# Top-k attention with two expert layers: full-row tail keys, transposed weights in place, four score buffers, one matrix fetched behind a gather

## The chip, the core and the metric

The kernel runs on one core of one Trainium2 chip. The metric is the device time of one execution in microseconds (us). The core has a matrix engine (TensorE, PE in the rows, with its weight loads as PEld), a vector engine (VectorE, DVE), an activation engine (ScalarE, ACT), a general engine (GpSimd, POOL) and a queue that issues most transfers (SyncE, SP). Each engine runs its own instructions in order and waits on semaphores for the others.

## The reference

```python
scores = q @ k^T / 8                      # 4 batches, 8 heads, 576 queries x 576 keys, 64 per head
scores = where(scores >= 32nd largest of the row, scores, -1e9)
x = softmax(scores) @ v                   # -> 2304 tokens x 512
g = clipped-quadratic(x @ w_in)           # 512 -> 2048
x = g @ w_out                             # 2048 -> 512
logits = x @ w_gate                       # 8 experts
# all (token, expert) pairs in falling order of logit; a token goes to the first
# expert that is not full (288 places each)
out[mask_e] = relu(x[mask_e] @ w1[e]) @ w2[e]
```

## The kernel before, in words

**First phase.** The work is cut into 80 pairs: for each of 4 batches, four blocks of 128 queries and one of 64, times four pairs of heads. `scores` multiplies queries by keys in PSUM bank `pS`; ScalarE copies the result to a score buffer `s` (a ring of three, `t_s`). `topk` finds the 32nd largest with eight-wide maxima on VectorE, and ScalarE and GpSimd turn the buffer into masked exponentials, in place. `values` transposes the weights: four 128x128 pieces for each head go through bank `pPT` into a buffer `pt` (ring of two); the last 64 keys of both heads and the reciprocal of the sums go through bank `pQ` into `tr` (ring of one). It then multiplies by the values: for each head (half of the 128 output rows) four matmuls over 128 keys (`v`) and one over the last 64 keys (`u`, on 64 rows of the array). VectorE scales the result into `xf` (ring of one), and ScalarE and GpSimd split it into a high and a low part in `XB`.

Between the pairs run 32 decodes of 64-bit weight words (`weights`, in the first 160 us), and, as soon as 256 tokens are ready, the two big matrices for each of nine blocks (`ffn_block`).

**Second phase.** `route` finds expert after expert: three rounds of counting on VectorE and TensorE (tiles `yb`, `I`, `ge`, `n`), then the places of the expert's tokens (`places`), which give the row numbers `idx`. Three indirect transfers (`gathers`) bring 96 rows each into `xg`. `expert` fetches the expert's first matrix (four tiles `raw`) and its second one (four more), splits each into a high part (ScalarE) and a low part (VectorE) in `W`, transposes the rows and multiplies. For the first expert, two blocks of tokens that come out of the last FFN block are added from `yo` instead of being gathered (`last_block`).

**Order.** All operations are recorded, and a planner with costs of its own (`Program.issue`) sets the order on each engine. So an edit of one operation can move others; at run time each engine keeps the planned order and waits.

Nearly all operations stand in the profile under line 267, that of the recorder; so rows are told apart by tiles.

Of the kernel before, what the change touches and what calls it, by code (L numbers as in the profile page):

```python
# [9 lines left out]
F32 = mybir.dt.float32  # L10
# [4 lines left out]
AF = mybir.ActivationFunctionType  # L15
# [32 lines left out]
NF, NM, NSM, NXF, NTR, NQR = 5, 2, 3, 1, 1, 2  # L48
# [230 lines left out]
def kernel(ctx: ExitStack, tc: tile.TileContext, qm, qt, kT, vm, vt,  # L279
# [85 lines left out]
    def first_phase(exact, actx):  # L365
# [18 lines left out]
        t_u = ring(4, [128, 2, D], F32, "u")  # L384
        t_qr = ring(NQR, [128, 2, 128], F32, "qr")
        t_q = ring(2, tiles=[part(8192 + 512 * i, 512).rearrange("p (z i x) -> p z i x", z=2, i=2) for i in range(2)])
        t_s = ring(3, tiles=s_tiles)
# [3 lines left out]
        t_pt = ring(2, [128, 4, 128], F32, "pt")  # L391
        t_tr = ring(NTR, [128, 2, 128], F32, "tr")
        t_xf = ring(NXF, [128, 128], F32, "xf")
# [50 lines left out]
        def weights(exact):  # L444
            raws = [stage[:, 1024 * i:1024 * i + 1024] for i in range(2)]
            raws += [t.rearrange("p a x -> p (a x)")[:, :1024] for t in (t_s(), t_s(), t_s())[1:]]
            t32s = [stage[:, 2048:2560], spare] + [t_pt().rearrange("p c x -> p (c x)") for _ in range(2)]
# [26 lines left out]
        def load_pair(b, p):  # L474
# [13 lines left out]
            Y.dma_start(out=u_t[:, 0, :], in_=vt[b, :, p])  # L488
            Y.dma_start(out=u_t[:64, 1, :], in_=vt[b, 64:, p])
# [134 lines left out]
        def values(b, j, p, r, s_sb, rinv, wide):  # L624
            P.rank = r + R_PV
            _, v_t, u_t = KV[b, p]
            tail, rb, acc = pQ[:, 0:128], pQ[:, 128:256], pQ[:, 256:384]
            full = j < 4
            w = 128 if full else 64
            pts = []  # L630
            for i in range(2 if full else 1):
                o_ = 64 * i
                with P.group():
                    for c in range(4):
                        T.transpose(pPT[:, 128 * c:128 * c + 128], s_sb[:, i, o_ + 128 * c:o_ + 128 * c + 128], ident)
                pt = t_pt()
                A.activation(pt.rearrange("p c x -> p (c x)"), pPT, AF.Copy)
                pts.append(pt)
            flat = s_sb.rearrange("p a x -> p (a x)")
            tr = t_tr()  # L640
            if full:
                A.activation(wide.rearrange("p (a x) -> p a x", a=2), rinv[:, :2].unsqueeze(2).to_broadcast([128, 2, 64]),
                             AF.Copy)
            with P.group():
                if full:
                    T.transpose(tail, flat[:, 512:640], ident)
                    T.transpose(rb, wide, ident)
                else:
                    T.transpose(tail[:64, :], flat[:, 512:576], ident)
                    T.transpose(rb, rinv[:, 0:1].to_broadcast([128, 128]), ident)  # L650
            if full:
                A.activation(tr.rearrange("p a x -> p (a x)"), pQ[:, :256], AF.Copy)
            else:
                A.activation(tr[:64, 0, :], tail[:64, :], AF.Copy)
                A.activation(tr[:, 1, :], rb, AF.Copy)
            for cs in ((0, 1), (2, 3, 4)):
                with P.group():
                    for c in cs:
# [10 lines left out]
            if full:  # L669
                V.tensor_tensor(out=xf, in0=acc, in1=tr[:, 1, :], op=ALU.mult)  # L670
            else:
                for h in range(2):
                    hs = slice(64 * h, 64 * h + 64)
                    V.tensor_tensor(out=xf[hs, :64], in0=acc[hs, :64], in1=tr[hs, 1, hs], op=ALU.mult)
            t0 = b * S + 128 * j
            c0 = 0
            while c0 < w:
                k, off = divmod(t0 + c0, BLK)
                n = min(w - c0, BLK - off)
                if k not in xT:  # L680
                    xT[k] = t_x()
                xh, xl = xT[k][:, 0, p, off:off + n], xT[k][:, 1, p, off:off + n]
                A.activation(xh, xf[:, c0:c0 + n], AF.Copy)
                G.tensor_tensor(out=xl, in0=xf[:, c0:c0 + n], in1=xh, op=ALU.subtract)
                c0 += n
# [80 lines left out]
        def routing_constants():  # L766
            raw = t_pt().rearrange("p c x -> p (c x)")
# [14 lines left out]

        if not exact:
# [21 lines left out]
        t_pt.reset()  # L805
        at, blk = 0.0, 0
        for b in range(B):
            for j in range(5):
                for p in range(NP):
                    s_sb, f = scores(b, j, p, at, exact)  # L810
                    rinv, wide = (topk_exact if exact else topk)(b, j, p, at, s_sb, f)
                    values(b, j, p, at, s_sb, rinv, wide)
# [18 lines left out]
    def second_phase(exact, rctx):  # L831
# [250 lines left out]
        def route(ph):  # L1082
# [77 lines left out]
            V.scalar_tensor_tensor(out=pos, in0=sc, scalar=pS[:, 1, 8:9], in1=tk, op0=ALU.add, op1=ALU.mult)  # L1160
# [6 lines left out]
        def places(ph, ei, pos):  # L1167
# [50 lines left out]
        def expert(ph):  # L1218
# [195 lines left out]
```

## Time and profile before

| | |
|---|---|
| median of 3 runs | 1151.74 us (1150.81 to 1154.38) |
| profiled execution, its own time | 1145.99 us |
| its span, first to last instruction | 1143.7 us |
| mean granted TensorE clock | 0.963 |
| busy: PE, PEld, DVE, ACT, POOL | 93%, 82%, 81%, 70%, 61% |

The profiled execution is one of its own and lies 5.75 us under the median of the timed runs. The busy shares are means over stages that differ: attention alone, attention with the FFN, routing, and experts.

### The profile page before, as it was taken

To read this page: it belongs to the slowest core of one execution; us is meant where nothing else is said; L and a number is where in the kernel's file an instruction comes from. 1 tells how busy PE (TensorE), PEld (TensorE's weight loads), DVE (VectorE), ACT (ScalarE), POOL (GpSimd) and SP (SyncE) were. 2 spreads that over 40 slices of the span, in tenths; PEclk is the share of its full clock that TensorE was granted. 3 is DMA by queue.
4 is the path that set the end of the run, shared out by engine and by line. 5 is a ranking of instruction groups with operands and counts; after the bars stand their busy time and mean duration, and the time that the engine had idled before them with its cause. 6 is when DMAs were issued, how large, how long until landed. Compare 5 with 4: busy or idle time off the path is not lost. (4 is left out here: it accounts for less than half of the span.)

```text
span 1143.7 us, 24385 instructions
## 1 busy us (share of the span) xinstructions
PE 1062.0 (93%) x8359; PEld 940.0 (82%) x8359; DVE 931.2 (81%) x2923; ACT 805.0 (70%) x1835; POOL 697.5 (61%) x872
## 2 busy tenths in 40 slices
PE   3677799999999999999999999999997999999995
PEld 2456588888888888898888888888976899999995
DVE  7899999889999999989899999984257997776430
ACT  8899987778888888877888988874313455445541
POOL 6988988977876988757688777763211152223111
PEclk9976599999999999999999999999988999999998
DMA  9744332352212352322134312212315664556500
GB/s 268 220 156 157 111 117 70 109 165 66 92 54 61 96 175 66 92 73 80 61 101 129 93 52 70 82 59 64 117 53 184 208 200 160 169 189 204 175 22 24
DMA packets 62197, 132.81 MB, mean 116 GB/s; under 512 B 15984, under 2 KB 24432, under 8 KB 62064
## 3 DMA queue, kind: packets, MB, share of 16 engines
q1 hardware_dynamic: 58992, 121.73, 33.8%
q0 software_dynamic: 3072, 9.44, 2.5%
q8 instruction: 67, 1.10, 0.4%
q14 instruction: 66, 0.54, 0.2%
HBM read 116.98 MB, written 14.16 MB: 115 GB/s over the span
## 5 line engine op out<-in xcount | busy, mean ns | idle before, releaser
L267 PE MATMUL pH<-XB,W 128*128 128x256 f32 (+1 forms) x2496 | 360.0, 291 | 0.7 <-DVE spare L267 0.3
L267 PEld LDWEIGHTS pH<-XB,W 128*128 128x128 f32 x2496 | 326.5, 189 | 9.7 <-issue 2.9
L267 DVE MAX8 m<-f 128x8 f32<-128x288 f32 x720 | 302.6, 449 | 2.2
L267 POOL TENSOR_TENSOR s<-s,f 128x576 f32<-128x576 f32 x144 | 204.3, 1430 | 30.0 <-ACT f L267 29.1
L267 DVE MATCH_REPLACE8 f<-m,f 128x288 f32<-128x288 f32 x432 | 190.7, 444 | 0.5 <-issue 0.3
L267 PE MATMUL pX<-W,XB 128*128 128x512 f32 x608 | 184.7, 411 | 0.7 <-ACT XB L267 0.7
L267 PE MATMUL pS<-XB 128*128 128x288 f32 (+2 forms) x672 | 145.2, 327 | 31.9 <-POOL XB L267 15.3
L267 POOL TENSOR_TENSOR XB<-stage,XB 128x512 fp32r<-128x512 f32 (+1 forms) x96 | 126.9, 1323 | 59.1 <-ACT XB L267 35.1
L267 PEld LDWEIGHTS pS<-XB 128*128 128x128 f32 x672 | 107.9, 203 | 52.4 <-DVE f L267 18.5
L267 ACT ACTIVATE s<-s,sm 128x576 f32<-128x576 f32 x144 | 111.3, 773 | 22.4 <-POOL s L267 21.3
L267 PEld LDWEIGHTS pX<-W,XB 128*128 128x128 f32 x608 | 107.7, 191 | 19.4 <-issue 2.9
L1210 POOL DMA_INDIRECT xg<-dram_x,idx x24 | 35.4, 1476 | 123.6 <-issue 49.4
L267 ACT ACTIVATE f<-s,t_all 128x576 f32<-128x576 f32 x144 | 108.2, 772 | 2.5
L267 ACT ACTIVATE s<-pS 128x576 f32<-128x576 f32 x144 | 92.7, 643 | 23.2 <-PE pS L267 22.8
L267 PE MATMUL pX<-XB,W 128*128 128x288 f32 x768 | 108.6, 297 | 0.0
L267 DVE TENSOR_TENSOR f<-pS,s 128x288 f32<-128x288 f32 x198 | 86.4, 450 | 22.5 <-ACT s L267 9.2
L267 DVE TENSOR_TENSOR W<-raw,W 128x1024 fp32r<-128x1024 f32 x64 | 76.8, 1218 | 33.5 <-ACT W L267 33.3
L267 PEld LDWEIGHTS pX<-XB,W 128*128 128x128 f32 x768 | 103.5, 188 | 0.0
L267 PE MATMUL pPT<-ident,s 128*128 128x128 f32 x576 | 92.8, 286 | 8.3 <-ACT s L267 6.8
L267 ACT ACTIVATE pt<-pPT 128x512 f32<-128x512 f32 x144 | 84.9, 589 | 17.5 <-PE pPT L267 17.1
L267 PE MATMUL pQ<-pt,v 128*64 128x128 f32 (+1 forms) x1280 | 91.7, 283 | 5.4 <-ACT tr L267 5.2
L1304 POOL DMA_INDIRECT out_dram<-yo,idx x24 | 26.9, 1120 | 109.8 <-ACT yo L267 106.3
(209 smaller groups left out, 1910.2 us busy)
## 6 DMA issues: line engine op xcount, KB each, us to landing
wl<-dram_wlo SPq DMA_DIRECT2D x64, 512.0 KB, 3.4
raw<-in_w_dram SPq DMA_DIRECT2D x64, 512.0 KB, 4.8
qr<-in_qm_dram SPq DMA_DIRECT2D x128, 64.0 KB, 2.4
stage<-in_w_in_dram SPq DMA_DIRECT2D x14, 512.0 KB, 4.2
stage<-in_w_out_dram SPq DMA_DIRECT2D x14, 512.0 KB, 3.3
stage<-in_kT_dram SPq DMA_DIRECT2D x48, 144.0 KB, 2.8
dram_wlo<-wl SPq DMA_DIRECT2D x8, 512.0 KB, 3.1
v<-in_vm_dram SPq DMA_DIRECT2D x16, 256.0 KB, 3.2
```

Of the source, the lines that this page charges most:

```text
L267: P.add(eng, lambda: fn(*args, **kw), cost, reads, writes, lat)
L1210: return nc.gpsimd.indirect_dma_start(out=xg[:, g, :], out_offset=None, in_=x2d[:, :], in_offset=bass.IndirectOffsetOnAxis(ap=idx[:, g:g + ...
L1304: st = nc.gpsimd.indirect_dma_start(out=out, out_offset=bass.IndirectOffsetOnAxis(ap=idx[:, g:g + 1], axis=0), in_=yo, in_offset=None)
```

## The change

It does the following:

- The last 64 keys' values `u` stand in a buffer of 128 rows, head 0 in the upper and head 1 in the lower half, with zeros between (written once by GpSimd). Their matmul goes over all 128 rows. For the blocks of 64 queries one more transpose puts the same weights on both halves.
- Transposed weights go back into the score buffer that they come from, `xf` too; `pt` and `xf` are gone. There are four score buffers (the fourth, `s_last`, also serves the first decodes and the constants), and two `tr`, each half as wide; one ScalarE copy of 256 columns becomes two of 128.
- The ten value matmuls of a pair are one group for the planner, no longer two.
- In `route`, one VectorE instruction comes in ahead of the running sum (`most`) and one behind the sum of the places goes (`tok`).
- The first expert's second matrix is fetched only when all three gathers of that expert have landed.

```diff
-        t_s = ring(3, tiles=s_tiles)
+        s_last = apool.tile([128, 2, S], F32, name="s3")
+        t_s = ring(4, tiles=s_tiles + [s_last])
...
-            Y.dma_start(out=u_t[:, 0, :], in_=vt[b, :, p])
-            Y.dma_start(out=u_t[:64, 1, :], in_=vt[b, 64:, p])
+            for h in range(2):
+                Y.dma_start(out=u_t[64 * h:64 * h + 64, h, :], in_=vt[b, 64 * h:64 * h + 64, p])
...
-            if full:
-                A.activation(tr.rearrange("p a x -> p (a x)"), pQ[:, :256], AF.Copy)
...
+                    if full:
+                        T.transpose(tail, flat[:, 512:640], ident)
+                        T.transpose(rb, wide, ident)
+                    else:
+                        T.transpose(tail, flat[:, 448:576], ident)
+                        T.transpose(tail[:64, :], flat[:, 512:576], ident)
+                        T.transpose(rb, rinv[:, 0:1].to_broadcast([128, 128]), ident)
+                A.activation(flat[:, 512:640], tail, AF.Copy)
+                A.activation(tr, rb, AF.Copy)
...
+                pt = flat[:, 640 * i:640 * i + 512]
...
-            for cs in ((0, 1), (2, 3, 4)):
-                with P.group():
...
-                            elif full:
-                                T.matmul(acc[hs, :w], u_t[hs, 0, :], tr[hs, 0, :], start=False, stop=True)
                             else:
-                                T.matmul(acc[hs, :w], u_t[:64, h, :], tr[:64, 0, hs], start=False, stop=True)
...
+                                T.matmul(acc[hs, :w], u_t[:, h, :], flat[:, 512:640] if full else flat[:, 512:640][:, hs],
+                                         start=False, stop=True)
...
-            xf = t_xf()
...
+                xf = flat[:, :128]
...
+            most = rt([128, NT], F32, "most")
+            V.tensor_scalar(most, tk, 2.0 * N * E, None, op0=ALU.mult)
...
-            tok = rt([96, 3], F32, "tok")
-            V.tensor_reduce(out=tok, in_=pS[:96, 1, :6].rearrange("p (a g) -> p g a", a=2), axis=AX, op=ALU.add)
-            V.tensor_scalar(idx, tok, N - 1.0, None, op0=ALU.min)
+            V.tensor_reduce(out=idx, in_=pS[:96, 1, :6].rearrange("p (a g) -> p g a", a=2), axis=AX, op=ALU.add)
...
-                P.add("sync", partial(fetch, raw, i // 4, i % 4), 1450, [ei[0:1, 0:1]], [raw], 2500)
+                P.add("sync", partial(fetch, raw, i // 4, i % 4), 1450, [ei[0:1, 0:1]] + [xg] * (early and i > 3), [raw], 2500)
```

**First place: TensorE, the value matmuls of the first pair.** Before, a planner's group of four matmuls (each stands as two records in a trace) is cut off from the group of six by other work. The number behind a tile's name is its buffer.

```order
L267 MATMUL pQ<-pt_138,v_118 64x128
L267 MATMUL pQ<-pt_139,v_118 64x128
L267 MATMUL pQ<-pt_138,v_118 64x128
L267 MATMUL pQ<-pt_139,v_118 64x128
L267 MATMUL pS<-XB 128x288 x4
L267 MATMUL pX_71<-ident,stage 128x128 x4
L267 MATMUL pQ<-pt_138,v_118 64x128
L267 MATMUL pQ<-pt_139,v_118 64x128
L267 MATMUL pQ<-pt_138,v_118 64x128
L267 MATMUL pQ<-pt_139,v_118 64x128
L267 MATMUL pQ<-tr_140,u_122 64x128 x2
L267 MATMUL pS<-XB 128x288 x2
```

With the change the same pair reads the score buffer itself, in one run.

```order
L267 MATMUL pQ<-ident,s_105 128x128
L267 MATMUL pQ<-ident,f_132 128x128
L267 MATMUL pS<-XB 128x288 x4
L267 MATMUL pX_71<-ident,stage 128x128 x4
L267 MATMUL pQ<-s_105,v_118 64x128 x8
L267 MATMUL pQ<-s_105,u_122 64x128 x2
```

What moved: in the order before, 20 of the 80 pairs are cut in two like this; in the order with the change none is.

**Second place: VectorE, between the first expert's second matrix and the second expert's running sum (`SC`).** Before, the low parts of that matrix (`W_96`, `W_98`) stand ahead of the third round of the search.

```order
L267 TENSOR_TENSOR W_96<-raw_9798,W_95 128x1024
L267 TENSOR_TENSOR W_96<-raw_9799,W_95 128x1024
L267 TENSOR_SCALAR ge_9757<-pQ 128x8
L267 TENSOR_TENSOR W_98<-raw_9800,W_97 128x1024
L267 TENSOR_REDUCE n_0_9759<-pPT 128x1
L267 TENSOR_SCALAR y_9751<-y_9752,n_0_9759 128x18
L267 TENSOR_TENSOR W_98<-raw_9801,W_97 128x1024
L267 COPY yb_9754<-y_9751 128x144
```

With the change the third of its four tiles (`raw_9887`) stands directly ahead of the sum.

```order
L267 TENSOR_TENSOR W_98<-raw_9887,W_97 128x1024
L267 TENSOR_TENSOR yc_9848<-C_9833,eh_9827 128x144
L267 TENSOR_TENSOR closed_9818<-closed_9818,eh_9827 128x8
L267 SCALAR_TENSOR_TENSOR ej_9854,ef_9856<-eh_9827,s_105 128x8
L267 TENSOR_REDUCE ch_9850<-yc_9848 128x18
L267 TENSOR_SCALAR cp_1_9852<-closed_9818 128x8
L267 TENSOR_SCALAR ei_9858<-ef_9856 128x1
L267 SCALAR_TENSOR_TENSOR tk_9829<-y_9838,n_1_9847,ch_9850 128x18
L267 TENSOR_TENSOR L_0_9821<-L_0_9821,cp_1_9852 128x144
L267 SCALAR_TENSOR_TENSOR pen_9819<-tk_9829,pen_9819 128x18
L267 TENSOR_SCALAR most_9861<-tk_9829 128x18
L267 SCALAR_TENSOR_TENSOR SC_9823<-tk_9829 128x18
```

What moved: the round is now ahead of the second matrix's first tile, but its result waits behind the third tile.

**Third place: TensorE, just ahead of the first expert's first matmul (`pH_69<-XB,W_91`).** Before, nothing of the second expert's sum stands there.

```order
L267 MATMUL pX_71<-s_107,yo_9796 128x288
L267 MATMUL pH_69<-XB,W_91 128x288 x2
L267 MATMUL pH_69<-XB,W_92 128x288
L267 LDWEIGHTS ones_f
L267 MATMUL pPT<-ge_9758,ones_f 128x8
```

With the change the product of the sum (`pS<-SC`) does.

```order
L267 LDWEIGHTS ones_f
L267 MATMUL pPT<-ge_9845,ones_f 128x8
L267 MATMUL pH_70<-s_107,yo_9883 128x288
L267 MATMUL pS<-s_107,yo_9883 128x288
L267 MATMUL pX_71<-s_107,yo_9883 128x288
L267 LDWEIGHTS s_105
L267 MATMUL pS<-SC_9823,s_105 128x1
L267 MATMUL pH_69<-XB,W_91 128x288 x2
```

What moved: two products that need VectorE's results (`ge`, `SC`) are now ahead of the first expert's first matmul on TensorE.

## Rows read from the trace of the kernel before

**Rows 1.** Stretches: length, busy us of each engine (instructions), clock, DMA share, GB/s.

```profile
core 0: us, PE busy (x) PEld busy (x) DVE busy (x) ACT busy (x) POOL busy (x), PEclk, DMA share, GB/s
40.00:160.00 120.00, 91.94 (x556) 73.21 (x556) 116.22 (x354) 114.48 (x297) 104.63 (x126) 0.74 0.45 144
160.00:760.00 600.00, 592.67 (x4714) 514.93 (x4715) 556.66 (x1881) 498.56 (x1176) 470.91 (x612) 1.00 0.29 90
904.00:1144.00 240.00, 226.71 (x1971) 221.10 (x1969) 142.53 (x365) 105.64 (x191) 56.20 (x66) 0.98 0.43 141
```

**Rows 2.** Waits from 837 us to the end: who for whom, us, times, longest.

```profile
PE pH L267 <- DMA xg<-dram_x,idx: 8.5, 5, 3.0
```

**Rows 3.** Timeline of TensorE: start us, us, operation, records; three places.

```profile
436.13 1.09 PE L267 MATMUL pQ<-pt,v 128*64 128x128 f32 x16
437.16 0.44 PE L267 MATMUL pQ<-tr,u 64*64 64x128 f32 x4
437.52 0.50 PE L267 MATMUL pX<-W,XB 128*128 128x512 f32 x1
...
482.75 0.66 PE L267 MATMUL pQ<-pt,v 128*64 128x128 f32 x8
483.34 0.53 PE L267 MATMUL pS<-XB 128*128 128x288 f32 x2
483.80 0.66 PE L267 MATMUL pQ<-pt,v 128*64 128x128 f32 x8
484.39 0.43 PE L267 MATMUL pQ<-tr,u 64*64 64x128 f32 x4
...
450.64 0.60 PE L267 MATMUL pPT<-ident,s 128*128 128x128 f32 x4
451.00 0.78 PE L267 MATMUL pS<-XB 128*128 128x288 f32 x4
451.61 0.39 PE L267 MATMUL pX<-W,XB 128*128 128x512 f32 x1
```

**Rows 4.** ScalarE's groups by shape, 160 to 760 us: busy us, mean ns.

```profile
L267 ACT ACTIVATE tr<-pQ 128x256 f32<-128x256 f32 x53 | 20.0, 377 | 1.7 <-PE pQ L267 1.7
L267 ACT ACTIVATE tr<-pQ 128x128 f32<-128x128 f32 x12 | 3.2, 264 | 0.0
```

**Rows 5.** GpSimd's first real work; the constants' transfer: KB, median us to landing.

```profile
8.42 1.28 POOL L267 TENSOR_TENSOR W<-pt,W 128x512 fp32r<-128x512 f32 x1 [7.97 <-ACT W L267]
...
pt<-in_consts_dram SPq DMA_DIRECT2D x1, 240.0 KB, 2.5
```

**Rows 6.** Timeline around the first expert's gathers, all engines.

```profile
862.44 5.81 SPq L1233 DMA_DIRECT2D raw<-in_w_dram  x4
865.43 1.77 POOL L1210 DMA_INDIRECT xg<-dram_x,idx  x1 [0.30 <-issue]
874.12 0.74 PE L267 MATMUL pH<-ident,xg 96*128 96x96 f32 x2 [3.03 <-DMA xg<-dram_x,idx]
879.14 1.22 DVE L267 TENSOR_TENSOR W<-raw,W 128x1024 fp32r<-128x1024 f32 x1
883.26 0.77 PE L267 MATMUL pH<-XB,W 128*128 128x288 f32 x3
```

**Rows 7.** Tile xg, all 24 gathers: from issue to landing.

```profile
DMA to landing us min/median/max: 3.4/5.9/11.9
```

**Rows 8.** A stretch behind that wait, columns as in the first group.

```profile
875.40:878.60 3.20, 3.20 (x12) 2.44 (x12) 1.26 (x2) 0.95 (x1) 0.00 (x0) 0.50 0.31 119
```

**Rows 9.** The second expert's first matrix: issue, and the cast of its third tile.

```profile
886.62 2.14 SPq L1232 DMA_DIRECT2D raw<-in_w_dram  x4
...
893.67 1.07 ACT L267 ACTIVATE W<-raw 128x1024 fp32r<-128x1024 f32 x1 [0.65 <-DMA raw<-in_w_dram]
```

**Rows 10.** TensorE at the second expert's gathered rows.

```profile
901.50 0.30 PE L267 MATMUL pH<-ident,xg 96*128 96x96 f32 x1 [0.64 <-DMA xg<-dram_x,idx]
903.33 0.30 PE L267 MATMUL pH<-ident,xg 96*128 96x96 f32 x1 [1.53 <-DMA xg<-dram_x,idx]
```

More of the change, by code (lines that the diff above doesn't have):

```diff
@@ L445, in weights @@
             raws = [stage[:, 1024 * i:1024 * i + 1024] for i in range(2)]
-            raws += [t.rearrange("p a x -> p (a x)")[:, :1024] for t in (t_s(), t_s(), t_s())[1:]]
-            t32s = [stage[:, 2048:2560], spare] + [t_pt().rearrange("p c x -> p (c x)") for _ in range(2)]
+            raws += [t.rearrange("p a x -> p (a x)")[:, :1024] for t in s_tiles[1:3]]
+            t32s = [stage[:, 2048:2560], spare] + [s_last.rearrange("p a x -> p (a x)")[:, a:a + 512] for a in (0, 512)]
             for n in range(32):
@@ L622, in first_phase, with transposed @@
         xT, late = {}, []
-        def values(b, j, p, r, s_sb, rinv, wide):
+        def transposed(b, j, p, r, s_sb, rinv, wide):
             P.rank = r + R_PV
-            _, v_t, u_t = KV[b, p]
-            tail, rb, acc = pQ[:, 0:128], pQ[:, 128:256], pQ[:, 256:384]
+            tail, rb = pQ[:, 0:128], pQ[:, 128:256]
             full = j < 4
[L629 to L632, printed above, removed]
-                with P.group():
[L634 to L638, printed above, removed]
             flat = s_sb.rearrange("p a x -> p (a x)")
@@ L643, in values, with last @@
                              AF.Copy)
-            with P.group():
-                if full:
[L646 to L651, printed above, removed]
-                A.activation(tr.rearrange("p a x -> p (a x)"), pQ[:, :256], AF.Copy)
-            else:
-                A.activation(tr[:64, 0, :], tail[:64, :], AF.Copy)
-                A.activation(tr[:, 1, :], rb, AF.Copy)
-            for cs in ((0, 1), (2, 3, 4)):
-                with P.group():
-                    for c in cs:
+            def last():
+                with P.group():
+                    if full:
[7 more added lines that the diff above has]
+                A.activation(tr, rb, AF.Copy)
+            if not full:
+                last()
+            pts = []
+            for i in range(2 if full else 1):
+                pt = flat[:, 640 * i:640 * i + 512]
+                with P.group():
+                    for c in range(4):
+                        T.transpose(pPT[:, 128 * c:128 * c + 128], pt[:, 128 * c:128 * c + 128], ident)
+                A.activation(pt, pPT, AF.Copy)
+                pts.append(pt.rearrange("p (c x) -> p c x", c=4))
+            if full:
+                last()
+            return pts, flat, tr
+        def values(b, j, ps, r, made):
+            P.rank = r + R_PV
+            full = j < 4
+            w = 128 if full else 64
+            accs = [pQ[:, 256 + 128 * n:384 + 128 * n] for n in range(2)]
+            with P.group():
+                for p, (pts, flat, tr), acc in zip(ps, made, accs):
+                    _, v_t, u_t = KV[b, p]
+                    for c in range(5):
                         for h in range(2):
@@ new lines, in values @@
+            t0 = b * S + 128 * j
+            for p, (pts, flat, tr), acc in zip(ps, made, accs):
+                xf = flat[:, :128]
+                if full:
+                    V.tensor_tensor(out=xf, in0=acc, in1=tr, op=ALU.mult)
+                else:
+                    for h in range(2):
+                        hs = slice(64 * h, 64 * h + 64)
+                        V.tensor_tensor(out=xf[hs, :64], in0=acc[hs, :64], in1=tr[hs, hs], op=ALU.mult)
+                c0 = 0
+                while c0 < w:
+                    k, off = divmod(t0 + c0, BLK)
+                    n = min(w - c0, BLK - off)
+                    if k not in xT:
+                        xT[k] = t_x()
+                    xh, xl = xT[k][:, 0, p, off:off + n], xT[k][:, 1, p, off:off + n]
+                    A.activation(xh, xf[:, c0:c0 + n], AF.Copy)
+                    G.tensor_tensor(out=xl, in0=xf[:, c0:c0 + n], in1=xh, op=ALU.subtract)
+                    c0 += n
@@ L781, in need @@
                 more[1] = next(more[0]) + 1
+        P.rank = -10.0
+        for u_t in us:
+            G.memset(u_t[64:, 0, :], 0.0)
+            G.memset(u_t[:64, 1, :], 0.0)
         if not exact:
@@ L811, in first_phase @@
                     rinv, wide = (topk_exact if exact else topk)(b, j, p, at, s_sb, f)
-                    values(b, j, p, at, s_sb, rinv, wide)
+                    made.append(transposed(b, j, p, at, s_sb, rinv, wide))
+                    values(b, j, (p,), at, made)
+                    made = []
                     at += 1.0 if j < 4 else 0.6
@@ L1159, in route @@
             pos = rt([128, NT], F32, "pos")
-            V.scalar_tensor_tensor(out=pos, in0=sc, scalar=pS[:, 1, 8:9], in1=tk, op0=ALU.add, op1=ALU.mult)
+            V.scalar_tensor_tensor(out=pos, in0=sc, scalar=pS[:, 1, 8:9], in1=most, op0=ALU.add, op1=ALU.min)
             places(ph, ei, pos)
```

28 lines of the change are left out of this document (5 added, 23 removed).

## The prediction

> **What bounds the kernel now.** First the stretches [rows 1]: the kernel changes its limit three times. From 40 to 160 us, while the weights are decoded, VectorE is busy 116.2 of 120 us and ScalarE 114.5, TensorE 92 at a mean clock of 0.74: work taken off TensorE there buys nothing. From 160 to 760 us (attention beside the FFN) TensorE is busy 592.7 of 600 us and VectorE 556.7: TensorE leads, VectorE has 43 us in hand. From 904 us to the end (the experts) TensorE is busy 226.7 of 240 us, idle mostly behind its last matmul; an earlier start of that stage ends the kernel earlier. Between them lies the one place where TensorE stands still for a transfer: it waits 8.5 us in five pieces for gathered rows [rows 2].
>
> **The value matmuls.** The timeline of TensorE shows what the 64-row matmuls cost [rows 3]. In an uncut pair the 16 full-row records take 436.13 to 437.16, 1.03 us; a run of 8 takes 482.75 to 483.34, 0.59 us. So 8 more records cost 0.44, 0.055 each, and what is over is paid on entering and leaving. The four 64-row records take 437.16 to 437.52, 0.36 us. Four more records of the full-row kind would take 0.22. So a pair gains 0.14 us.
>
> A cut pair pays for entering twice: 2 x 0.59 - 1.03 = 0.15 us; and its guest, two score matmuls, takes 483.34 to 483.80, 0.46 us, where an undisturbed four take 0.61 (451.00 to 451.61), so 0.15 more: 0.30 us for a cut. By the order 20 pairs are cut before and none after; about 18 of them lie in the stage in which TensorE leads, and 70 of the 80 pairs. Gain there: 70 x 0.14 + 18 x 0.30 = 15.2 us. The added transpose of the 14 short blocks in it, four transposes taking 0.36 us (450.64 to 451.00), takes back 14 x 0.09 = 1.3. TensorE is relieved of 13.9 us.
>
> How much of it reaches the end? At most all; nothing, if VectorE (which gives up no instruction) is the true limit. VectorE's 43 us of idle time say that it follows TensorE's pace more than it sets it, but not everywhere: I take three quarters, 10.5 us.
>
> A rule speaks against this step. The Trainium skill, "TensorEngine Tiling (Array Packing)", sections Overview and When to Use Tiling, has it that a contraction of 64 rows or fewer should run as row tiles, for up to twice the speed. The trace disagrees: four 64-row records at 0.36 us are dearer than four full-row ones at 0.22, since the two heads run side by side in either form. By the rule the padded records would take twice 0.36 us, and the sum would be 25 us worse instead of 10 better.
>
> **The buffers.** A score buffer was free once its weights were transposed; now it is held until GpSimd has split the result, but there are four. I count it at 1 us of gain: between 0 and what VectorE's idle time leaves after the matmuls' part, some 20 us at the very most, and a loss if the longer hold outruns the fourth buffer (a rival below). ScalarE's one copy of 377 ns becomes two of at most 264 [rows 4]: 0.15 us more for each of 64 pairs, hidden by ScalarE's 101 idle us in the long stage, but not before 160 us, where some 9 pairs could cost 1.4 us; I count nothing, as VectorE is the fuller there. GpSimd's eight memsets lie in the 8 us in which it waits for its first operand [rows 5]; without that cover they would be a few tenths each. The `u` transfers become smaller and stay two for each pair of heads. New is a wait at the end of attention: the constants land in the fourth buffer, which the last pair now holds, and VectorE's casts of them, with the last FFN block's clipping behind them, wait 2.5 us for that transfer [rows 5]. Between 0 and 2 us; I take 0.5, as TensorE has the previous block's products to do.
>
> **The held fetch.** Around the first expert [rows 6] SyncE issues the second matrix at 862.44 us, GpSimd its third gather at 865.43, and TensorE gets that gather's rows only at 874.12. Over all 24 gathers a landing takes 3.4 us at best and 5.9 in the median [rows 7]. Without the second matrix beside it I take 4.2 us, nearer to the lower, since only the first matrix's last tiles still flow: landing at 869.6 (869 to 871.3 by the two bounds). So 4.5 of the 8.5 us of waiting go. But the second matrix starts only then, and VectorE's and TensorE's new order (second and third place above) puts the running sum of the next expert behind its third tile and the first expert's first matmul behind that sum. What that takes is shown by a burst of the same size that runs alone: issued at 886.62, the cast of its third tile starts 7.05 us later [rows 9]. So here: cast at 876.7, done at 877.7, low part (1.22 us [rows 6]) by 879.0, then eleven small VectorE operations and a first subtraction (an estimate: 1.9 us, somewhat over one and a half such low parts), 880.9, first matmul at 881 instead of 883.26. Of the 4.5 us, 2.3 are left.
>
> Then the clock. Behind the long wait TensorE ran at 1.2 GHz, the lower of its two levels (0.50), until 878.6 [rows 8], and it was full again when the first expert began. Now its idle time lies later, just ahead of that expert, and a drop to the same level would fall on dense work: 6.8 us at half clock cost 3.4 us, none cost nothing; I take 1.5. At the second expert's rows TensorE waits 0.64 and 1.53 us [rows 10]; that expert's search is about 5 us ahead of before while TensorE is only 2 ahead, so I drop these 2.2 us. Sum of the part: -2.3 + 1.5 - 2.2 = -3.0; bounds -8.5 (all waits of [rows 2] gone) and +3 (low clock, and the matrix landing late). The added `most` and the removed `tok` are one small VectorE operation each way on the same chain, under 0.2 us each and eight of either, behind TensorE's dense work: nothing.
>
> **The sum.** -10.5 - 1 + 0.5 - 3.0 = -14 us. Against the profiled execution's own 1145.99 us: 1132. It lies 5.75 us under the median of the runs, so for the median: 1151.74 - 14 = 1138 us. Within 0.3% (3.5 us) is what a measurement of this kernel can hardly tell from no change.
>
> **The rivals.**
> - *VectorE is the limit from 160 to 760 us.* For it: 93% busy. Against: TensorE has 7 us of idle time there, VectorE 43. The Trainium skill, "Perfetto Trace Analysis", section Identifying the Most-Contended Engine, speaks for it too: TensorE's headroom is to be read from weight loads, not from matmul time. By weight loads TensorE is 86% busy [rows 1], less than VectorE. Then TensorE's savings become waits, and some 1 us of the matmuls' part and the fetch's 3.0 remain: 1148 us. Chance 0.14.
> - *The fourth buffer frees VectorE.* If the score ring and not only TensorE held VectorE up, another 10 us of its idle time go: 1128 us. For it: three buffers for a pair's whole path from scores to transposes. Against: the order on TensorE puts the scores no further ahead than before. Chance 0.12.
> - *The hold on the second matrix costs more than the gather gains.* The upper bound above, +3: 1144 us. For it: the third tile ahead of the sum. Chance 0.12.
> - *The longer hold of a buffer outruns the fourth one: slower.* The pairs' order now needs GpSimd's last split of a pair before the fourth next pair's scores. Each us by which that comes late stops VectorE for the same time, for it has only these scores to do. Against 14 us of gain it decides from 0.2 us a pair on; at 0.25 us in 80 pairs, 20 us: 1158. Against it: one more buffer is 9 us more room in the long stage (600 us for some 65 pairs). Chance 0.04.
> - *Full rows cost double,* as by the first rule: 70 x (0.72 - 0.36) = 25 us instead of a gain of 10 from the matmuls: 1174 us. The rows above speak against it. Chance 0.01.
>
> **How the numbers follow.** The forecast, 1138 with 1131 to 1145 of its own, has 0.57. Range for 8 in 10: down to the fourth-buffer case, up to VectorE as the limit: 1127 to 1149. Faster by over 0.3%: the forecast, the buffer's case, most of the fetch's and half of VectorE's, 0.57 + 0.12 + 0.09 + 0.07 = 0.85; within 0.3%: 0.03 + 0.07 = 0.10; slower 0.05.
>
> **What would show it.** Right: the value matmuls of a pair stand as 20 records in about 1.25 us without a change of pace at the last four; the stage between the decodes and the last FFN block is 8 to 15 us shorter, with VectorE's busy share in it up from 93% to about 95%; the first expert's gathers land near 869.6 less what the first phase gained, and its first matmul starts about 2 us earlier relative to the gathers' issue; no wait at the second expert's rows. Wrong: new idle time of TensorE from 160 to 760 us as large as the matmuls' gain; ScalarE stopped for a tile of the second matrix with TensorE idle or at half clock behind it for more than 8 us; GpSimd's splits as the releaser of the scores' copies.

## The result, and the profile after

The changed kernel takes 1142.74 us (median of 5 runs, 1139.32 to 1143.89), the kernel before on the same chip 1151.74 us (5 runs): that is 9.0 us faster by the medians. The ratio on record is 0.9908, 95% interval 0.9882 to 0.9934, or 10.6 us (7.6 to 13.6); the comparisons below go by such ratios. The profiled execution of the changed kernel took 1143.89 us (span 1142.1), only 2.1 less than the profiled one of before. That gap between 2 and 9 us turns out to be part of the answer.

The long stage of [rows 1], in the changed kernel:

```profile
160.00:760.00 600.00, 588.21 (x4778) 521.69 (x4775) 556.08 (x1896) 507.98 (x1236) 475.27 (x614) 1.00 0.29 90
```

From 160 to 760 us TensorE (first busy column) fell from 592.7 to 588.2 us, VectorE (third) stayed at 556. By the forecast VectorE's share should have risen.

The value matmuls themselves became what was said of them. The timeline of TensorE for an uncut pair, columns as in [rows 3]:

```profile
437.01 1.09 PE L267 MATMUL pQ<-s,v 128*64 128x128 f32 x16
437.93 0.39 PE L267 MATMUL pQ<-s,u 128*64 128x128 f32 x4
438.25 1.20 PE L267 MATMUL pX<-W,XB 128*128 128x512 f32 x4
```

The 20 records take 437.01 to 438.25, 1.24 us (forecast 1.25, before 1.39). This pair is a typical one: in the long stretch defined below, the median of 66 pairs is 1.24 us, and before that of 50 uncut pairs was 1.39. Only a third of the 0.15 us lies at the last four records (0.32 us in place of 0.36); the rest lies ahead of them (0.92 in place of 1.03).

**A better ruler than fixed stretches.** Three events can be found in every trace: the first score copy of the 16th pair, the first expert's running sum on TensorE (`pS<-SC`), and the same for the fourth expert. They cut an execution into a start, a long stretch, the first three experts, and a rest. Here are the long stretch and the three experts for a second profile of the kernel before, an execution of 1152.48 us:

```profile
193.04:856.51 663.47, 655.02 (x5204) 569.89 (x5203) 572.61 (x1929) 506.88 (x1184) 469.73 (x606) 0.99 0.28 87
856.51:938.24 81.73, 72.66 (x593) 64.61 (x593) 63.56 (x182) 32.40 (x50) 19.77 (x15) 0.87 0.59 191
```

and for the changed kernel:

```profile
195.61:853.71 658.10, 644.76 (x5216) 571.64 (x5214) 567.61 (x1928) 512.36 (x1238) 471.12 (x608) 0.99 0.28 88
853.71:930.51 76.80, 66.48 (x595) 61.00 (x594) 63.05 (x183) 32.20 (x50) 17.50 (x15) 0.96 0.62 203
```

The long stretch repeats from execution to execution: 663.56, 663.47 and 663.58 us in three profiles with the order of before, 658.10 and 658.09 in two of the changed kernel. (`a_nohold` below, with the same order on VectorE in this stretch, has 659.1, and 3.4 us more at the lower clock.) So differences of 2 us can be read there, where the times of whole runs scatter by 4 to 9 us. The rest repeats within 2 us. What scatters is the first three experts: 75.6 us in the first profile of before, 81.73 in the second. The profile on which the forecast was built was an execution with a short one.

All profiles by this ruler (us; "VectorE busy" and "idle" are of the long stretch), with the median and the ratio to before of the run's own chip:

| kernel | start | long | VectorE busy | idle | 3 experts | rest | median | ratio (95%) |
|---|---|---|---|---|---|---|---|---|
| before, first profile | 192.6 | 663.6 | 572.7 | 90.8 | 75.6 | 212.0 | 1151.74 | |
| b_again | 193.0 | 663.5 | 572.6 | 90.9 | 81.7 | 212.0 | 1149.41 | 0.9995 (0.9982–1.0008) |
| b_hold | 193.7 | 663.6 | 572.8 | 90.8 | 72.5 | 212.0 | 1143.67 | 0.9950 (0.9934–0.9966) |
| b_values | 201.7 | 657.1 | 572.2 | 85.0 | 79.1 | 212.0 | 1149.33 | 1.0001 (0.9985–1.0017) |
| b_no_u | 191.1 | 652.9 | 569.1 | 83.8 | 79.9 | 212.7 | 1140.27 | 0.9896 (0.9870–0.9923) |
| changed, first profile | 195.6 | 658.1 | 567.6 | 90.5 | 76.8 | 211.6 | 1142.74 | 0.9908 (0.9882–0.9934) |
| a_again | 193.7 | 658.1 | 567.6 | 90.5 | 77.3 | 212.8 | 1141.40 | 0.9909 (0.9885–0.9934) |
| a_nohold | 193.6 | 659.1 | 567.6 | 91.4 | 74.8 | 211.7 | 1141.23 | 0.9942 (0.9921–0.9963) |
| a_u64 | 195.0 | 660.6 | 570.0 | 90.6 | 74.2 | 211.8 | 1141.82 | 0.9915 (0.9894–0.9936) |
| a_s3 | 195.6 | 676.3 | 574.8 | 101.6 | 77.9 | 213.2 | 1164.58 | 1.0108 (1.0082–1.0134) |
| a_pe | 194.6 | 665.4 | 568.9 | 96.5 | 72.7 | 211.4 | 1145.58 | 0.9968 (0.9951–0.9985) |
| a_dve | 198.0 | 668.8 | 586.6 | 82.2 | 77.1 | 212.0 | 1158.17 | 1.0053 (1.0032–1.0074) |
| a_fold | 196.1 | 652.8 | 559.9 | 92.9 | 73.4 | 211.3 | 1132.37 | 0.9846 (0.9832–0.9860) |
| a_clip | 191.8 | 659.0 | 565.1 | 93.9 | 74.4 | 211.3 | 1136.81 | 0.9882 (0.9865–0.9900) |

The runs are of several chips, on which the kernel before took 1149.4 to 1152.6 in the median; so kernels are compared by ratios, and a difference of ratios is turned into us with 1150.

### The profile page after: what moved, and what is told of

Its sections match the earlier page's. It is cut to its first block, busy times and chain, and to the rows that moved or that the text cites. A ratio compares the mean times of both kernels' runs of the same rounds, so it can differ in the third digit from the quotient of the medians.

```text
span 1142.1 us, 24518 instructions
## 1 busy us (share of the span) xinstructions
PE 1053.5 (92%) x8375; PEld 950.1 (83%) x8375; DVE 924.8 (81%) x2923; ACT 810.7 (71%) x1899; POOL 702.3 (61%) x880
## 4 chain that ended last, share of the span: by engine, by line
PE 65%; DVE 14%; ACT 8%; POOL 4%; issue 4%; DMA 3%; another core or an unknown queue 0%; SPq 0%; POOLq 0%; DVEq 0%; ACTq 0%
PE pH L267 24%; PE pX L267 23%; PE pS L267 7%; PE pQ L267 7%; DVE f L267 5%; DVE m L267 4%; PE pPT L267 4%; ACT s L267 3%; POOL XB L267 2%; DMA raw<-in_w_dram 2%; DVE stage L267 1%; ACT stage L267 1%; POOL s L267 1%; ACT XB L267 1%; ACT spare L267 1%
## 5 line engine op out<-in xcount | busy, mean ns | idle before, releaser
L267 PE MATMUL pH<-XB,W 128*128 128x256 f32 (+1 forms) x2496 | 365.2, 294 | 1.1 <-DVE XB L267 0.8
L267 PEld LDWEIGHTS pH<-XB,W 128*128 128x128 f32 x2496 | 330.3, 192 | 11.5 <-issue 5.7
L1228 POOL DMA_INDIRECT xg<-dram_x,idx x24 | 38.3, 1596 | 122.0 <-DVE idx L267 48.1
L267 ACT ACTIVATE s<-pS 128x576 f32<-128x576 f32 x144 | 92.9, 645 | 19.1 <-PE pS L267 17.8
L267 ACT ACTIVATE XB<-pH 128x288 fp32r<-128x288 f32 x94 | 37.2, 409 | 81.4 <-PE pH L267 65.8
L267 ACT ACTIVATE s<-pPT 128x512 f32<-128x512 f32 x144 | 85.3, 592 | 10.9 <-PE pPT L267 10.4
```

Source lines behind the costliest of these rows:

```text
L267: P.add(eng, lambda: fn(*args, **kw), cost, reads, writes, lat)
L1228: return nc.gpsimd.indirect_dma_start(out=xg[:, g, :], out_offset=None, in_=x2d[:, :], in_offset=bass.IndirectOffsetOnAxis(ap=idx[:, g:g + ...
```

## The experiments

### Which part brings the gain

**b_values**: before, with the matmul part alone. The padded `u`, the extra transpose and:

```diff
-            for cs in ((0, 1), (2, 3, 4)):
+            for cs in ((0, 1, 2, 3, 4),):
...
-                                T.matmul(acc[hs, :w], u_t[hs, 0, :], tr[hs, 0, :], start=False, stop=True)
+                                T.matmul(acc[hs, :w], u_t[:, h, :], tr[:, 0, :], start=False, stop=True)
```

> The kernel before with only the matmul part of the change: the last 64 keys on all 128 rows with zeros between (and the extra transpose for the short blocks), and the ten value matmuls of a pair in one group; buffers, routing and fetches as before. Forecast's theory (TensorE leads from 160 to 760 us, three quarters of its relief reach the end): 10.5 us faster than before, about 1141 us, ratio 0.991. Rival (VectorE is the limit there): about 1 us, 1150.5, ratio 0.999, with TensorE's busy time in that stretch some 14 us lower and its waits for VectorE's and ScalarE's results as much higher. Rival (the gain of the whole change comes from the buffers): no difference either, and the whole gain shows only with the four buffers.

Measured: no gain (1.0001). The ruler says why it is not a plain no: the long stretch is 6.4 us shorter, with VectorE's idle time down from 90.8 to 85.0, but the start is 9 us longer (201.7 against 192.6). The planner, given other operations, laid out the decodes in another order. TensorE's busy time in the long stretch is 8.0 us lower (647.1 against 655.0), so most of the relief arrived there, although the clock was at its lower level, 1.2 GHz, for 17.1 us of it (6.8 each from 326.1 and 653.7, 3.4 from 841.5 us), against 6.8 us in the kernel before. So something like the forecast's effect exists in this order, at 6 us and not 10.5, and was paid for elsewhere.

**b_hold**: before, with the held fetch alone.

```diff
-                P.add("sync", partial(fetch, raw, i // 4, i % 4), 1450, [ei[0:1, 0:1]], [raw], 2500)
+                P.add("sync", partial(fetch, raw, i // 4, i % 4), 1450, [ei[0:1, 0:1]] + [xg] * (early and i > 3), [raw], 2500)
```

> The kernel before with only the held fetch of the first expert's second matrix. Forecast's theory: 3.0 us faster, 1148.7, ratio 0.997; the third gather lands 4.2 us after its issue instead of 8.7, the first expert's first matmul starts about 2.3 us earlier after that issue. Rival (the hold is what brought most of the measured 9 us): 6 us or more faster, ratio below 0.995. Rival (the hold costs): 1154, ratio 1.003.

Measured: 0.9950, 5.8 us (3.9 to 7.6), near the rival that the hold brings most. Everything but the first three experts takes as long as before (within them the planner orders some operations anew). The third gather's rows are used 3.5 us after its issue (866.30 and 869.81; 4.2 expected), and the first expert's first matmul comes 15.9 us after that issue in place of 17.8. Against the first profile of before the three experts are 3.1 us shorter, the forecast's 3.0; against the second one 9.3. Its 8 runs lie within 2.8 us (1142.38 to 1145.20), the 31 runs of before beside it within 9.2 (1145.03 to 1154.24): the hold takes away a scatter.

**a_nohold**: the changed kernel with that line as before.

> The changed kernel without the held fetch. Forecast's theory: 3.0 us slower than the changed kernel, about 1145.7 us, ratio to before 0.995. If the hold is most of the gain: 1149 or more, ratio above 0.997. If the hold brings nothing: 1142.7, ratio 0.991. Its third gather should again take 8 to 9 us to its rows' use.

Measured: 0.9942, so the rest of the change brings 6.7 us (4.3 to 9.1), and the hold on top of it 3.8 (difference of ratios 0.0033, about as uncertain as it is large). Its third gather's rows are used 6.0 us after the issue (861.61 and 867.60), not the 8 to 9 that were expected. Its 12 runs spread over 10.8 us again.

**a_again**: the changed kernel itself, on another chip.

> The changed kernel itself, again, beside the three that follow. If the hold and the rest add up as the first experiments say (5.8 us of 1150 for the hold alone, 6.7 for the rest without it), it stands at a ratio of 0.989 to the kernel before, 1138 to 1139 us on that chip; if the hold is worth little on top of the rest, at 0.994. With the hold its runs should lie within 4 us of each other, against 9 to 11 without it.

Measured: 0.9909, the first result again; its six runs lie within 3.2 us. 5.8 and 6.7 would sum to 12.5; 10.5 is inside what they leave open.

**a_u64**: the changed kernel with the tail keys back on 64 rows.

```diff
-                                T.matmul(acc[hs, :w], u_t[:, h, :], flat[:, 512:640] if full else flat[:, 512:640][:, hs],
+                                T.matmul(acc[hs, :w], u_t[hs, h, :], flat[hs, 512:640] if full else flat[hs, 512:640][:, hs],
```

> The changed kernel with only the matmul of the last 64 keys put back on 64 rows (buffers, one group and held fetch stay): TensorE gets 0.14 us for each of 80 pairs, 11 us in all. The forecast's theory (three quarters of TensorE's time reach the end): 8 us above the changed kernel, ratio to before 0.998. VectorE leads and TensorE's time counts a third, as the doubled and the dropped matmuls gave: 3 to 4 us above it, ratio 0.994. The full rows are worth nothing in this order: ratio 0.991.

Measured: 0.9915 against 0.9909, nothing that can be told apart by the runs. The ruler tells more: the long stretch is 2.5 us longer. TensorE is busy 652.1 us in it in place of 644.8, and idle 8.5 in place of 13.3: of 7.3 us that the full rows and their order take off TensorE, 4.8 come back as waits. The order matters here, since the planner laid out all engines anew for this run (VectorE's order differs from near its start on), so the run does not price the full rows alone.

**a_s3**: the changed kernel with three score buffers.

```diff
-        t_s = ring(4, tiles=s_tiles + [s_last])
+        t_s = ring(3, tiles=s_tiles)
```

> The changed kernel with three score buffers instead of four (the buffers are still overwritten in place and so held longer). If the fourth buffer brings what the change gains in the first phase, this one is 6 us or more slower than the changed kernel and, with the longer hold, perhaps slower than before: ratio 0.995 to 1.01. If the buffers hardly matter (the forecast counted 1 us): within 2 us of the changed kernel.

Measured: 1.0108, 23 us above the changed kernel, in another order. So with the edit in place the fourth buffer is worth some 20 us. What the buffer's longer life costs was not measured by itself; that it costs about as much is argued from VectorE's idle time, which the two together leave where it was (90.8 before, 90.5 after). By that reading the fourth buffer is the price of the edit in place, no gain.

### Which engine's time counts

**a_pe**: TensorE gets more to do, in an unchanged order.

```diff
+                                if c == 0:
+                                    P.grp["calls"].append(partial(nc.tensor.matmul, acc[hs, :w], v_t[:, c, hs], rhs, start=True, stop=True))
                                 T.matmul(acc[hs, :w], v_t[:, c, hs], rhs, start=(c == 0), stop=False)
```

> The changed kernel with the first value matmul of each head issued twice (the second overwrites the first): four more records for each of the 80 pairs, 0.055 us each, 17.6 us of TensorE's time, with the planned order of all engines unchanged. TensorE leads: three quarters or more of it reach the end, 1156 to 1160 us, that is 13 to 17 us above the changed kernel, ratio to before 1.004 to 1.008. VectorE leads: TensorE has slack, and not more than 4 us arrive, 1143 to 1147, ratio 0.991 to 0.995; TensorE's busy time from 160 to 760 us then rises by about 15 us with no later end of the stage.

Measured: 0.9968, 6.8 us (3.4 to 10.2) above the changed kernel for 17.6 us of work: 0.4 us for each. Neither theory's number. The parts are less even: the long stretch is 7.3 us longer, and the three experts are 4.1 us shorter, for want of a stop that the last section shows and that has no part in the value matmuls.

**b_no_u**: TensorE gets less to do, in the order of before; the last 64 keys' share of the result is left out.

```diff
-                                T.matmul(acc[hs, :w], v_t[:, c, hs], rhs, start=(c == 0), stop=False)
+                                T.matmul(acc[hs, :w], v_t[:, c, hs], rhs, start=(c == 0), stop=(c == 3))
...
+                            if c == 4:
+                                P.grp["calls"].pop()
```

> The kernel before without the matmuls of the last 64 keys, which are left out of the result; the planned order of all engines is that of before, so TensorE loses 0.36 us in each of 80 pairs, 29 us, and nothing else moves. TensorE leads (the forecast): three quarters, 20 us or more, reach the end, ratio 0.982. VectorE leads: 2 us or less, ratio 0.998 or more. Both in turn: TensorE's relief counts only where it leads for the moment, 6 to 10 us, ratio 0.991 to 0.995.

Measured: 0.9896, 12.0 us (8.9 to 15.0) for 29 us of work: 0.4 again. The long stretch gives 10.6 of it.

**a_dve**: VectorE gets more to do.

```diff
             for i in range(n):
                 V.max(out=m[:, i, 40:48], in_=m[:, i, 24:40])
+                P.ops[-1]["calls"].append(partial(nc.vector.max, out=m[:, i, 40:48], in_=m[:, i, 24:40]))
```

> The changed kernel with VectorE's last small maximum (128x16 to 128x8, 163 ns as recorded) issued twice for each row half of each pair: 144 more instructions, some 12 to 23 us of VectorE's time, with the planned order unchanged. VectorE leads: nearly all of it reaches the end, 12 us or more above the changed kernel. TensorE leads (the forecast): VectorE has slack, 4 us or less. Both in turn: about half.

Measured: 1.0053, 16.6 us (12.8 to 20.3) above the changed kernel. By the trace VectorE's busy time up to the first sum rose by 24 us (start 182.1 against 176.8, long stretch 586.6 against 567.6), so 0.7 us for each over the whole run, less than the whole. It looks like more than TensorE's 0.4, but 5.3 of the 24 us lie in the start, where VectorE is the fuller engine; in the long stretch it is 10.7 us for 19.0.

**a_fold** and **a_clip**: VectorE gets less to do.

```diff
-FOLD_DVE = (0, 4, 4, 4)
+FOLD_DVE = (0, 2, 2, 2)
```

> The changed kernel with half of VectorE's second folds (the minimum of a row's halves, 128x288, 0.45 us) moved to GpSimd: 27 of them, 10 to 12 us off VectorE, and 2 x 0.81 us each, 44 us, onto GpSimd, which is idle 125 of 600 us in the long stage. The planner makes its order anew. VectorE leads: 5 to 11 us below the changed kernel, ratio to before 0.981 to 0.987. TensorE leads (the forecast): no gain, ratio 0.991. GpSimd becomes the next limit, since the fold's result then comes 1.2 us later: ratio above 0.993.

```diff
-LOW_ACT, CLIP_ACT, R_UK = (), (0,) * 9, {}
+LOW_ACT, CLIP_ACT, R_UK = (), (2,) * 8 + (0,), {}
```

> The changed kernel with two of the eight clips of each of the first eight FFN blocks done by ScalarE (two extra operations each) instead of VectorE: 16 of VectorE's 128x512 clips, 0.68 us as recorded, 9 to 11 us off VectorE, about 18 us onto ScalarE, which is idle 92 of 600 us in the long stage. The planner makes its order anew. VectorE leads: 5 to 10 us below the changed kernel, ratio to before 0.982 to 0.987. TensorE leads (the forecast): ratio 0.991. ScalarE becomes the next limit: above 0.993.

Measured: a_fold 0.9846, 7.2 us (4.0 to 10.5) below the changed kernel and the fastest of all, 1132.37 us (18 us below before, 16 to 19). Its long stretch, whose VectorE and GpSimd times are to be set beside the changed kernel's 567.61 and 471.12 above:

```profile
196.09:848.91 652.82, 642.46 (x5210) 571.04 (x5209) 559.88 (x1900) 509.82 (x1238) 509.54 (x660) 0.99 0.28 88
```

GpSimd took 38 us more without becoming the limit. The Trainium skill, "Perfetto Trace Analysis", section Optimizing Scalar/DVE Operations, warns that moving work between VectorE and GpSimd may not help, as they share a port; here it did. a_clip: 0.9882, 3.1 us below the changed kernel, about as uncertain as it is large, between the theories: in the long stretch VectorE's busy time fell by 2.5 us only, in part for a reason that the last section gives.

**b_again**: the kernel before, profiled a second time.

> The kernel before itself. Ratio 1.000. The first profile of it was of an execution 5.75 us under the median; if the runs differ by how the first experts' rows land beside the unheld matrix, this profile differs from the first one by several us between the first expert's sum and the fourth one's, and by 2 us or less ahead of it and behind it.

Measured: 0.9995, and a profile 6.5 us longer than the first (span 1150.2 against 1143.7), of which 6.1 lie in the first three experts and 0.4 ahead of them.

## Why the prediction was right, and where it was not

The time was right (1138 forecast, 1142.7 and a ratio of 0.991 measured, inside 1127 to 1149); two of its terms were wrong in opposite directions, the matmuls' too large and the held fetch's too small. That they partly made up for each other is luck.

**"How much of it reaches the end? ... three quarters, 10.5 us": this step failed; about half arrived.** The mechanism of the matmuls held (1.24 us a pair, no pair cut). The relief was somewhat smaller than forecast: in the long stretch TensorE's busy time fell by 10.3 us (655.02 to 644.76), not 13.9, and the records of `u` show 65 pairs from 160 to 760 us where the forecast counted 70. But the stretch became only 5.4 us shorter, since TensorE's idle time in it rose from 8.4 to 13.3 us. TensorE's 592.7 of 600 busy us were read as the limit and VectorE's idle time as room. What a microsecond of either engine is worth there can be read from the three runs in which work was added or dropped and the order kept, a_pe, b_no_u and a_dve:

```profile
194.58:860.02 665.44, 656.37 (x5483) 586.02 (x5481) 568.90 (x1928) 512.76 (x1237) 470.20 (x608) 0.99 0.28 87
191.06:843.98 652.92, 637.53 (x4931) 557.93 (x4930) 569.11 (x1929) 505.27 (x1184) 469.56 (x606) 0.99 0.28 88
197.99:866.76 668.77, 648.22 (x5208) 571.00 (x5207) 586.57 (x2044) 512.96 (x1239) 471.39 (x608) 0.99 0.27 86
```

Against the changed kernel's row, a_pe has 11.6 us more of TensorE and is 7.3 longer; against the row of before, b_no_u has 17.5 less and is 10.6 shorter; a_dve has 19.0 more of VectorE and is 10.7 longer than the changed kernel. That is 0.63, 0.60 and 0.56 us for each. (TensorE's busy times are modelled by the profile; with the forecast's own prices for the 65 pairs in the stretch, 14.3 and 23.4 us, its two are 0.51 and 0.45.) Within this stretch neither engine clearly leads. The 0.4 and 0.7 of the whole runs are not a like comparison, for the reasons given at a_pe and a_dve, and because the 17.6 and 29 us of TensorE's work include that of the start, where TensorE waits for the others anyway. About half of what is added to one engine becomes waiting of the other: VectorE's idle time rises by 6.0 us in a_pe, TensorE's by 7.2 in a_dve. So of the rivals, "VectorE is the limit" is too strong in the same way as the forecast; by its 1 us for the matmuls b_no_u could not have gained 10.6.

Where the planner moves the order, the share varies: 6.4 of 8.0 us arrived in b_values, 2.5 of 7.3 lie between a_u64 and the changed kernel. Where the 5.8 us of VectorE's idle time went that b_values saved and the changed kernel did not is not settled: one group, the full rows, the buffers and the new order were not tried apart.

**Where the long stretch's 5.4 us came from is open between two accounts.** By the shares above, 10.3 us off TensorE are worth some 6, which would be enough. But seen from VectorE the gain did not come from waits: its idle time is the same, and its busy time is 5.1 us lower, with the same instructions. Of this 3.5 us are fifteen small instructions, which clear parts of a query tile (`XB<-ones_f`; a sixteenth lies in the start). The view of one tile, shortest, median and longest in ns, for the kernel before (second profile):

```profile
L267 DVE TENSOR_SCALAR XB<-ones_f x16: 276/564/1461, 187.7 to 759.6; 128x256 fp32r<-128x256 bf16 x16
```

and for the changed kernel:

```profile
L267 DVE TENSOR_SCALAR XB<-ones_f x16: 270/294/1283, 189.6 to 756.5; 128x256 fp32r<-128x256 bf16 x16
```

Their sum is 11.5 us before and 6.8 after; in the long stretch it is 10.1 and 6.6. No step of the forecast spoke of them, and nothing in the diff touches them: the planner's new order put them at other moments. At a_dve's 0.56 these 3.5 us are worth some 2 (an estimate). No run undid them alone, so how the 5.4 us divide between TensorE's relief, this accident of order, and what the buffers and the rest of the order took back is not shown. That the clearings count at all is supported by a_u64, which has 1.6 us more of them in the long stretch than the changed kernel, and is 2.5 us longer there at the same idle time of VectorE (but it has 7.3 us more of TensorE too). In a_clip they are 10.5 us, and take back 3.7 of the 10.8 us that its sixteen clips lasted on VectorE.

**The held fetch: the mechanism was right, the size too small.** Forecast -3.0 us; b_hold measured -5.8. In the changed kernel:

```profile
862.71 1.31 POOL L1228 DMA_INDIRECT xg<-dram_x,idx  x1 [0.30 <-issue]
...
866.17 0.46 PE L267 MATMUL pH<-ident,xg 96*128 96x96 f32 x2 [1.09 <-DMA xg<-dram_x,idx]
866.88 1.64 SPq L1251 DMA_DIRECT2D raw<-in_w_dram  x3
...
878.75 0.18 PE L267 MATMUL pS<-SC,s 128*128 128x1 bf16 x1 [3.74 <-DVE SC L267]
879.09 1.32 PE L267 MATMUL pH<-XB,W 128*128 128x288 f32 x6 [0.17 <-DVE XB L267]
```

The third gather's rows are used 3.5 us after its issue (4.2 forecast, 8.7 before [rows 6]). The new order then gives part of it back as foreseen: TensorE waits 3.74 us for the sum behind the third tile, and the first matmul comes 25.4 us after the first expert's sum, in place of 27.1 in the first profile of before: 1.8 us earlier (2.3 forecast). No row of the second expert's gathers is waited for (2.2 us dropped, as foreseen). What was mis-sized is the clock behind the wait that the hold removes. The first profile had 6.8 us at half clock there (a part of it in [rows 8]). The second one of before, in stretches of 4 us:

```profile
868.00:872.00 4.00, 0.46 (x2) 0.30 (x2) 2.43 (x3) 1.79 (x3) 0.00 (x0) 1.00 1.05 314
872.00:876.00 4.00, 2.86 (x24) 2.37 (x25) 1.95 (x3) 2.20 (x3) 0.00 (x0) 0.53 0.78 255
876.00:880.00 4.00, 4.00 (x17) 3.49 (x16) 2.08 (x4) 0.73 (x1) 0.00 (x0) 0.50 0.06 19
...
884.00:888.00 4.00, 4.00 (x34) 3.06 (x33) 1.91 (x6) 1.65 (x4) 0.00 (x0) 0.77 0.00 0
```

TensorE is almost idle from 868 to 872 and then runs at 1.2 GHz (0.50) until about 886, some 14 us. Behind the second expert's gathers, for which it waits 2.5 us, it runs at that level for another 6.8 us (906.4 to 913.2). Over the three experts it is busy 72.66 us, 6.5 more than in the first profile, which is as much as the two executions differ. The time at half clock within the three experts is 6.8, 20.5, 17.1 and 17.1 us in the four profiles with the unheld fetch of before (first, second, b_values, b_no_u), and 6.8 in b_hold and in both of the changed kernel. So the step that was mis-sized is "I take 1.5" for the clock, together with the 5.75 us that were added back as if they were constant: the forecast took its price from an execution in which the low clock was short. By the difference of 17.1 and 6.8 at half speed the hold saves some 5 us there (an estimate) where the forecast counted a loss.

**The other terms.** Buffers, -1: neither shown nor refuted; by a_s3 the fourth buffer gives some 20 us, and what the longer hold costs is known only as part of the whole. That the longer hold outruns the ring, the rival on the slower side, shows with three buffers: VectorE is idle 101.6 us in a_s3, and ScalarE's copies into the score buffers wait 2.9 us for GpSimd's splits, a wait that the changed kernel does not have. The wait for the constants, +0.5, did not come: VectorE's casts, which waited 1.74 us for them before, wait for nothing in the changed kernel. "The fourth buffer frees VectorE" is out: VectorE's idle time did not fall. "The hold costs more" is out (b_hold). "Full rows cost double" is out (a_u64). "The stage ... is 8 to 15 us shorter, with VectorE's busy share up": 5.4 us, and the share is 86% in both. The start is up to 3 us longer in the profiles of the changed kernel (193.7 and 195.6 against 192.6 and 193.0); ScalarE's two copies, which the forecast left at nothing, may be that, but it was not tested.

## What to carry to other kernels

Where two engines are each over 85% busy, neither "leads": ask for the price of a microsecond of each, by adding or dropping work in an unchanged order, before counting a saving at three quarters, and read it in the stretch itself: over whole runs the two engines seemed to differ here (0.4 and 0.7), in the long stretch they did not (0.6 each). A planner's new order can move as much time as the edit (9 us in the start of b_values, 4.7 us in sixteen clearing instructions), so compare by stretches that repeat from run to run. And if one profile lies well under the median of the runs, find the stretch in which it was lucky before pricing an edit there: a change that removes scatter shows in the median more than in one trace.

## What the runs showed of the hardware that was not expected

**A small VectorE instruction lasts as long as GpSimd's.** In the second profile of before:

```profile
583.36 1.41 POOL L267 TENSOR_TENSOR XB<-stage,XB 64x576 fp32r<-64x576 f32 x1
583.46 1.45 DVE L267 TENSOR_SCALAR XB<-ones_f 128x256 fp32r<-128x256 bf16 x1 [0.52 <-PE pS L267]
```

and in the changed kernel:

```profile
189.61 0.27 DVE L267 TENSOR_SCALAR XB<-ones_f 128x256 fp32r<-128x256 bf16 x1
189.63 1.40 POOL L267 TENSOR_TENSOR XB<-stage,XB 128x512 fp32r<-128x512 f32 x1
```

The clearing that starts 0.10 us behind a GpSimd operation ends 0.14 us behind its end (584.77 and 584.91), after 1.45 us; the one that starts 0.02 us ahead of one takes 0.27. The others in these two traces that start inside a GpSimd operation end 0.15 to 0.16 us behind its end too, all but one (at 384.44 us in the changed kernel). So the busy record holds the wait, and no view of waits shows it. The Trainium skill, "SBUF — State Buffer", section Who interferes with whom, gives the rule: a VectorE copy, cast or tensor-scalar operation in a two-port mode and a GpSimd operation exclude each other, whichever comes first, for its whole length. These rows agree where GpSimd comes first; whether the clearing runs in such a mode, and whether GpSimd waits when it comes second, they do not show. VectorE's maxima are not stretched: one that starts at 189.17, inside a GpSimd operation that lasts from 188.83 to 189.63, takes 0.45 us like the others. No run was made with the clearing moved to ScalarE; by the rows up to 6.8 - 16 x 0.27 = 2.5 us of VectorE's time are left to gain there in the changed kernel, and more in a_clip.

**VectorE stops for 3 us with no releaser in the profile.** In the changed kernel's third expert:

```profile
919.00 0.68 PE L267 MATMUL pQ<-C,I 128*128 128x8 bf16 x18
...
922.98 0.17 DVE L267 TENSOR_SCALAR ge<-pQ 128x8 bf16<-128x8 f32 x1 [3.23 <-remote]
923.20 0.17 PE L267 MATMUL pPT<-ge,ones_f 128*128 128x8 bf16 x1 [2.62 <-DVE ge L267]
```

`ge` needs the product that TensorE had done by 919.7, yet it starts 3.3 us later, and the profile names no instruction that released it. The DMA engines were full at that time (share 1.01 from 919 to 923), and TensorE, idle for 2.6 us, came back at 0.63 of its clock from 923 to 927. In a_pe, whose second phase is the same, `ge` waited for nothing like it and its three experts took 72.7 us in place of 76.8. It is not one execution's accident: a_again, a_dve and a_s3 have the same stop ahead of the same instruction, 3.3 to 3.4 us each, and their three experts took 77.1 to 77.9 us; a_nohold, a_u64, a_pe, a_fold and a_clip do not have it and took 72.7 to 74.8. So some 3 us are left in the changed kernel that the hold doesn't reach. What stops VectorE is open. One candidate is untested: the trace records a 16 KB transfer of an instruction queue that starts 1.1 to 1.3 us into the stop in three of the four profiles, and 1.1 us ahead of it in a_dve, and that ends 0.9 to 2.3 us before `ge` starts.
